# Gate transposes at three to a step, block sums behind two maxima and on GpSimd, in an attention and expert kernel on one core

## The chip, the core and the metric

The kernel runs on one core of a Trainium2 chip. The metric is device time in microseconds of one execution, median of several runs. TensorE (PE) does matrix products and transposes, VectorE (DVE) and ScalarE (ACT) read their results out of PSUM, GpSimd (POOL) works on SBUF alone, and SyncE (SP) issues nearly all loads and stores, in order. Every engine works through its own instructions in program order and waits on semaphores for the others.

## The reference

Two batches of eight heads, 768 positions, head size 64. Each position attends to a band of its neighbours and to 24 blocks of 32 positions, of which the keys are the maximum over the block and the values the mean. The result, 1536 rows of 512, goes through a gate that picks two of eight experts for each row, through these experts, and then through a second feed-forward block.

```python
k_sum = k.reshape(B, H, nb, block, D).max(axis=3)
v_sum = v.reshape(B, H, nb, block, D).mean(axis=3)
mask_l = np.abs(pos[:, None] - pos[None, :]) < window
scores_all = np.concatenate([np.where(mask_l, scores_l, -1e9), scores_s + np.log(block)], axis=-1)
attn = softmax(scores_all) @ np.concatenate([v, v_sum], axis=2)      # x: 1536 x 512
noisy = x @ w_gate + np.log1p(np.exp(x @ w_noise)) * noise           # top two of eight
for each expert e: out[rows of e] += weight * (relu(x[rows] @ w1[e]) @ w2[e])
h = relu(out @ w_in); result = (s * h * h + b) @ w_out
```

## The kernel before

**Attention.** Two heads make a unit `u` (eight units, four to a batch), half of the positions of a unit make a group `n` (16 groups, `u, g = divmod(n, 2)`). The loop over `n` is a software pipeline, one group a step. In step `n` TensorE gets, in this order, the scores of group `n` (`stage_s`, here S(n)), the transposes of the probabilities of group `n-2` (`stage_pt`, pt) and the product with the values of group `n-3` (`stage_pv`, pv). VectorE takes the row maximum of S(n) (L737) and negates and scales it (L738), ScalarE the six exponentials (`stage_exp`, L741) and the copies of the transposes out of PSUM (L755). VectorE normalises pv into the rows of x, `xs[b]` (L771, L773). After a batch's last unit each group's rows are also stored to `x_d` by SP (L776).

For the unit to come, VectorE takes the block maxima of K (`block_max`, L707), GpSimd lays out the windows of K (L703) and places the maxima (L711). `make_vsum` (L688) sums the blocks of `vT` on VectorE; the sums `vz` ride along in `stage_pt` as a seventh transpose (L754), and `place_vsum` puts them into the value tile `VW` (ACT L692, POOL L693). The loads K, Q, vT of unit `u+2` and VW of `u+1` are issued by SP in `extra(n)` at the end of every even step; each waits until its buffer is free.

**PSUM.** `bank()` hands out two banks (`mbk`) in turn to pt (two a step) and to all other short work. The scores alternate between `bk23` and `bk45`; the gate's logits (`gps`) are columns 400 to 495 of `bk23`.

**Gate.** `gate_t(b, i)` transposes 128 rows of x (four transposes, L783) into a bank and copies them to a tile `xt` (ACT L789 or DVE L787). `gate_m(b, k)` multiplies three of these with the gate weights (24 matmuls, L799) and copies the 96x128 result `lt` (ACT L803). `gate_z(b, k)` transposes it back into `bk23` (L806). The table `GATE` places the work of batch 0 in steps 10 to 12, and `TAIL` names that of batch 1 (g, m, z).

**Routing.** `top2`, `ranks`, `slots` (lines 172 to 268) turn logits into slots: many small VectorE operations, for batch 0 spread by `ROUTE` over steps 12 to 15. `first_ids` (d.0, L283 on TensorE, L876 and L877 on VectorE) makes the ids of unit 0's rows, and GpSimd gathers them from `x_d` (L547). `first_x` (x.0, x.1) transposes 128 of these rows each (L528) and splits them into a high (L530) and a low part (L531).

**Tail.** The string `TAIL` is the written order of everything from the last three groups' pt and pv to the first matmuls of unit 0: l1.i and l2.i are the two expert products of step i (L501, L522), s.i splits weights (ACT L411, then L494 and L495 on GpSimd or VectorE), t, r, o, i are the routing of batch 1, whose ids let unit 1's rows be gathered (p.0 to p.3 transpose them). From unit 1 on the loop `step(n)` runs products on TensorE to the end.

Of the kernel before, what the change touches and what calls it, by code (L numbers as in the profile page):

```python
# [9 lines left out]
F32 = mybir.dt.float32  # L10
# [5 lines left out]
AF = mybir.ActivationFunctionType  # L16
# [3 lines left out]
DRAM = bass.MemoryType.DRAM  # L20

EDGE_CAP = 256
GATE_EV = {(0, 1): 1, (0, 3): 1, (0, 5): 1, (1, 0): 1, (1, 3): 1, (1, 4): 1}
CHUNK_AT = (3, 7, 12)
SPLIT_AT = (6, 8)
SPLIT_DVE = {8: 1, 9: 1, 4: 0}
ROUTE = {12: 2, 13: 3, 14: 7, 15: 6}
GATE = {(10, 0): 't0', (10, 1): 't1', (10, 2): 't2', (11, 0): 't3 m0', (11, 1): 't4', (11, 2): 't5 z0', (12, 0): 'm1', (12, 1): 'z1'}
XT_B = 4
TAIL = ("pt.1 pv.0 d.0 pt.2 pv.1 g.0 g.1 pv.2 g.2 g.3 m.0 x.0 g.4 z.0 x.1 s.2 g.5 m.1 l1.0 z.1 s.3 l1.1 t.0 s.4 l2.0 l1.2 u.0 c.3 l2.1 s.5 "  # L30
        "r.0 o.7 l2.2 o.2 s.6 l1.3 l1.4 l2.3 o.2 s.7 l1.5 l2.4 c.4 i.0 l1.6 s.8 l1.7 s.9 l2.6 l2.5 p.0 p.1 e.0 p.2 p.3 l2.7 l1.8")
MID_CAPS = (464, 440, 424, 416, 392, 368, 344)

# [2 lines left out]
def kernel(ctx: ExitStack, tc, q, k, v, vt_in, w_gate, w_noise, noise, w1, w2,  # L36
# [8 lines left out]
    P = 128  # L45
# [490 lines left out]

    def gather_x(u):
        if u == 0:
            t = ap_.tile([P, 2, Dm], F32, name="xg0")
            rows = [t[:, i] for i in range(2)]  # L540
        else:
            t = sp.tile([P, 4, Dm], F32, name="xg", bufs=2)
            rows = [t[:, i] for i in range(4)]
        xg[u] = rows
        for st in range((caps[u] + P - 1) // P):
            w = min(P, caps[u] - st * P)
            nc.gpsimd.indirect_dma_start(  # L547
                out=rows[st][0:w], out_offset=None, in_=x_d[0:S if u == 0 else N, :],
                in_offset=bass.IndirectOffsetOnAxis(ap=ids_i[0:w, 4 * u + st:4 * u + st + 1], axis=0))
# [228 lines left out]
    xt_of = {}  # L778

    def gate_t(b, i):  # L780
        xp = bank()
        for t in range(DT):
            nc.tensor.transpose(xp[:, t * P:(t + 1) * P], xs[b][:, i, t * P:(t + 1) * P], ident)  # L783
        xt = ap_.tile([P, DT, P], F32, name="xt", bufs=XT_B)
        xt_of[b, i] = xt
        if GATE_EV.get((b, i), 0):
            nc.vector.tensor_copy(xt.rearrange("p t n -> p (t n)"), xp)  # L787
        else:
            nc.scalar.activation(xt.rearrange("p t n -> p (t n)"), xp, AF.Copy)  # L789


    gps = bk23[:, :, 400:400 + 96].rearrange("p k (i e) -> p k i e", e=32)
# [2 lines left out]
    def gate_m(b, k):  # L795
        ps = bank()[0:96, 0:P]
        for t in range(DT):
            for j in range(3):
                nc.tensor.matmul(ps[32 * j:32 * j + 32], wgn[:, t], xt_of[b, 3 * k + j][:, t], start=t == 0,  # L799
                                 stop=t == DT - 1)  # L800
        lt = ap_.tile([96, P], F32, name="lt", bufs=2)
        lt_of[b, k] = lt
        nc.scalar.activation(lt, ps, AF.Copy)  # L803

    def gate_z(b, k):
        nc.tensor.transpose(bk23[:, k, 400:400 + 96], lt_of[b, k], ident[0:96, 0:96])  # L806
# [388 lines left out]
```

## Time and profile before

| | us |
|---|---|
| median of 3 runs (690.10 to 690.83) | 690.42 |
| the profiled execution | 686.93 |
| its span, first to last instruction | 685.2 |
| TensorE busy (95%) | 653.4 |
| VectorE busy (63%) | 434.4 |
| ScalarE busy (52%) | 355.6 |
| GpSimd busy (24%) | 164.4 |

Times in the trace are microseconds from the start of the span. A group L737 is what line 737 of the kernel issues. "idle before" is the time in which the engine had nothing to do ahead of the instruction, and the arrow names what ended it. The granted clock (PEclk) is the share of TensorE's 2.4 GHz. The span has an attention part up to about 71 us, a tail up to about 85, unit 0 with the routing of batch 1 up to about 119, and then matrix products.

### The profile page before, as it was taken

The numbers are of one execution on the slowest core, as the hardware profiler recorded it, in microseconds if no ns is written. First come the engines' busy times: TensorE is split into PE (matmuls) and PEld (weight loads), VectorE is DVE, ScalarE is ACT, GpSimd is POOL, SyncE is SP. The second block draws the span as 40 slices with busy tenths as digits, with TensorE's granted clock in tenths as the row PEclk, the third lists the DMA queues.
The fourth block names the chain that finished last, engine by engine and source line by source line (L and its number), as shares of the span: only waits on it lengthen the run. The fifth ranks groups of instructions, "written<-read, shape, count | busy, mean of one in ns | idle before, by whom it ended". The sixth has DMA issues, their size and how long they took to land.

```text
span 685.2 us, 11202 instructions
## 1 busy us (share of the span) xinstructions
PE 653.4 (95%) x4236; PEld 571.8 (83%) x4236; DVE 434.4 (63%) x771; ACT 355.6 (52%) x660; POOL 164.4 (24%) x182
## 2 busy tenths in 40 slices
PE   4997689999999999999999999999999999999996
PEld 4776577889999999999898887888888888888884
DVE  5877466467776676677767666788555565554542
ACT  4866334455445555555555575566444554544432
POOL 5652467004041131303131174502400000000000
PEclk9999989999999999999999999999999999999999
DMA  8994504946566566566666642510410000100001
GB/s 338 378 329 169 186 26 139 354 136 207 183 191 205 172 230 202 183 220 226 204 230 214 223 124 80 163 34 31 124 63 0 1 0 1 63 0 1 0 1 66
DMA packets 58408, 97.58 MB, mean 142 GB/s; under 512 B 6695, under 2 KB 33319, under 8 KB 58347
## 3 DMA queue, kind: packets, MB, share of 16 engines
q1 hardware_dynamic: 54203, 83.62, 35.7%
q0 software_dynamic: 4144, 13.18, 6.8%
q8 instruction: 35, 0.57, 0.4%
q14 instruction: 26, 0.21, 0.1%
HBM read 83.61 MB, written 13.17 MB: 141 GB/s over the span
## 4 chain that ended last, share of the span: by engine, by line
PE 90%; DVE 4%; ACT 2%; DMA 1%; issue 1%; POOL 0%; SPq 0%; ACTq 0%; DVEq 0%
PE sbk L501 40%; PE bk L522 25%; PE bk L923 14%; PE mbk L528 2%; PE bk L768 2%; PE mbk L751 2%; PE mbk L522 1%; PE bk L726 1%; PE mbk L954 1%; DMA xl<-in_vT_dram 1%; ACT sm L741 1%; PE mbk L799 1%; DMA xg<-x_d,ids_i 1%; PE mbk L783 1%; DVE xs L773 0%
## 5 line engine op out<-in xcount | busy, mean ns | idle before, releaser
L501 PE MATMUL sbk<-xh,w 128*128 128x512 f32 (+8 forms) x960 | 280.0, 357 | 0.0
L501 PEld LDWEIGHTS sbk<-xh,w 128*128 128x128 f32 x960 | 176.5, 189 | 19.6 <-ACT xh L530 0.4
L501 PE MATMUL sbk<-xl,w 128*128 128x512 f32 (+8 forms) x480 | 171.0, 356 | 0.2 <-DVE xl L531 0.2
L522 PE MATMUL bk<-w,hh 128*128 128x512 f32 (+2 forms) x512 | 160.9, 396 | 0.0
L411 ACT ACTIVATE w<-r 128x512 fp32r<-128x512 f32 x140 | 80.7, 624 | 91.4 <-PE bk L923 56.9
L522 PEld LDWEIGHTS bk<-w,hh 128*128 128x128 f32 (+2 forms) x512 | 93.4, 188 | 17.9
L461 POOL TENSOR_TENSOR cl<-cl,cp 128x512 f32<-128x512 f32 x32 | 41.3, 1290 | 249.1 <-DVE cp L460 231.1
L522 PE MATMUL bk<-w,hl 128*128 128x512 f32 (+2 forms) x256 | 100.6, 393 | 0.0
L501 PEld LDWEIGHTS sbk<-xl,w 128*128 128x128 f32 x480 | 90.9, 189 | 10.3 <-DVE xl L531 0.5
L923 PE MATMUL bk<-hh,w 128*128 128x464 f32 (+4 forms) x320 | 96.4, 362 | 0.0
L494 DVE TENSOR_TENSOR w<-r,w 128x512 fp32r<-128x512 f32 x64 | 44.2, 690 | 35.2 <-ACT w L411 34.7
L512 ACT ACTIVATE yr<-sbk 128x512 f32<-128x512 f32 x48 | 28.7, 597 | 71.3 <-PE sbk L501 71.3
L517 DVE SCALAR_TENSOR_TENSOR hl<-yr,sb_in,hh 128x512 fp32r<-128x512 f32 x48 | 40.0, 833 | 36.0 <-ACT hh L514 36.0
L513 DVE SCALAR_TENSOR_TENSOR yr<-yr,sb_in 128x512 f32<-128x512 f32 x48 | 36.0, 750 | 41.9 <-ACT yr L512 41.9
L923 PEld LDWEIGHTS bk<-hh,w 128*128 128x128 f32 x320 | 59.8, 188 | 2.5
L514 ACT ACTIVATE hh<-yr,sb_in 128x512 fp32r<-128x512 f32 x48 | 34.8, 725 | 45.9 <-DVE yr L513 45.9
L486 DVE TENSOR_TENSOR w<-wres,w 128x1024 fp32r<-128x1024 f32 x36 | 44.1, 1224 | 22.0 <-ACT w L485 22.0
L522 PEld LDWEIGHTS bk<-w,hl 128*128 128x128 f32 (+2 forms) x256 | 48.0, 187 | 11.5 <-DVE hl L517 0.8
L923 PE MATMUL bk<-hl,w 128*128 128x464 f32 (+4 forms) x160 | 56.9, 356 | 0.0
L505 ACT ACTIVATE hh<-sbk 128x256 fp32r<-128x256 f32 (+7 forms) x72 | 34.5, 480 | 40.0 <-PE sbk L501 37.6
L506 DVE SCALAR_TENSOR_TENSOR hl<-sbk,hh 128x256 fp32r<-128x256 f32 (+7 forms) x72 | 38.9, 541 | 15.5 <-ACT hh L505 15.3
L485 ACT ACTIVATE w<-wres 128x1024 fp32r<-128x1024 f32 x39 | 41.3, 1058 | 14.3 <-PE bk L522 9.6
(186 smaller groups left out, 802.4 us busy)
## 6 DMA issues: line engine op xcount, KB each, us to landing
r<-in_moe_w_dram SPq DMA_DIRECT2D x72, 512.0 KB, 4.6
c<-in_moe_w_in_dram SPq DMA_DIRECT2D x16, 512.0 KB, 3.8
c<-in_moe_w_out_dram SPq DMA_DIRECT2D x16, 512.0 KB, 3.7
VW<-in_v_dram SPq DMA_DIRECT2D x8, 780.0 KB, 8.0
y_d<-yr SPq DMA_DIRECT2D x23, 256.0 KB, 2.3
kT<-in_k_dram SPq DMA_DIRECT2D x8, 384.0 KB, 6.8
qT<-in_q_dram SPq DMA_DIRECT2D x8, 384.0 KB, 8.1
xl<-in_vT_dram SPq DMA_DIRECT2D x8, 384.0 KB, 7.3
```

The source lines that it names most:

```text
L411: nc.scalar.activation(dst, src, AF.Copy)
L461: nc.gpsimd.tensor_tensor(out=lf, in0=lf, in1=pw.bitcast(F32), op=OP.mult)
L485: nc.scalar.activation(v2[:, 0], w, AF.Copy)
L486: eng.tensor_tensor(out=v2[:, 1], in0=w, in1=v2[:, 0].bitcast(F32), op=OP.subtract)
L494: eng.tensor_tensor(out=v4[:, 2], in0=a, in1=v4[:, 0].bitcast(F32), op=OP.subtract)
L501: nc.tensor.matmul(ps, wgt[:, t], x[:, t], start=i == 0, stop=i == 3 * DT - 1)
L506: nc.vector.scalar_tensor_tensor(out=hl, in0=ps, scalar=0.0, in1=hh.bitcast(F32), op0=OP.max, op1=OP.subtract)
L513: nc.vector.scalar_tensor_tensor(out=r2, in0=r, scalar=sb_in[:, 0:1], in1=r, op0=OP.mult, op1=OP.mult)
L514: nc.scalar.activation(hh, r2, AF.Identity, bias=sb_in[:, 1:2])
L517: nc.vector.scalar_tensor_tensor(out=hl, in0=r2, scalar=sb_in[:, 1:2], in1=hh.bitcast(F32), op0=OP.add, op1=OP.subtract)
L522: nc.tensor.matmul(a, g, wgt, start=first and j == 0, stop=last and j == 2)
L923: nc.tensor.matmul(a[:, 0:C], wgt[:, c], x[:, 0:C], start=f == 0 and j == 0, stop=last and j == 2)
```

## The change

**Transposes.** `gate_t(n)` now transposes, for one group, the 128 columns of one unit: three transposes (one for each 128 rows of the group) into three quarters of a bank, and one 128x384 copy into `XT[b]`, on VectorE for odd groups, on ScalarE for even ones. It stands at the end of step `n+4` for groups 0 to 11, and in the tail as v.0 to v.3 for groups 12 to 15 (v.2's copy goes to VectorE). `XT[0]` is a tile of its own; `XT[1]` is the memory of `xs[0]`, so its writers wait for `x_d`'s stores of batch 0. `gate_m` reads `XT` and copies `lt` on VectorE. In `GATE` the products of batch 0 stand in steps 11 and 12, the second gate_z behind pv and the new transposes of step 12.

**Start.** In steps 0 and 1 the maxima and exponentials come right behind the scores, and `make_vsum(0)` follows the second maximum. `load_vT(2)` goes from step 0 to step 1.

**Block sums of units 6 and 7.** GpSimd adds halves in place, five `tensor_tensor` of 24x16, 24x8, 24x4, 24x2 and 24x1 elements a row.

**Tail.** x.0 and x.1 come earlier, x.0 ahead of pv(15) (pv.2); l1.0 comes ahead of m.1 and z.1. The gathered rows of unit 0 go into `kw[0]` instead of a tile of their own.

```diff
-GATE = {(10, 0): 't0', (10, 1): 't1', (10, 2): 't2', (11, 0): 't3 m0', (11, 1): 't4', (11, 2): 't5 z0', (12, 0): 'm1', (12, 1): 'z1'}
-TAIL = ("pt.1 pv.0 d.0 pt.2 pv.1 g.0 g.1 pv.2 g.2 g.3 m.0 x.0 g.4 z.0 x.1 s.2 g.5 m.1 l1.0 z.1 s.3 l1.1 t.0 s.4 l2.0 l1.2 u.0 c.3 l2.1 s.5 "
+GATE = {(11, 1): 'm0', (11, 2): 'z0', (12, 1): 'm1', (12, 2): 'z1'}
+TAIL = ("pt.1 v.0 pv.0 d.0 pt.2 v.1 pv.1 x.0 v.2 pv.2 m.0 x.1 z.0 v.3 s.2 l1.0 m.1 z.1 s.3 l1.1 t.0 s.4 l2.0 l1.2 u.0 c.3 l2.1 s.5 "
...
-            t = ap_.tile([P, 2, Dm], F32, name="xg0")
+            t = kw[0].rearrange("p j c -> p (j c)")[:, 0:2 * Dm].rearrange("p (i d) -> p i d", d=Dm)
...
-        nc.vector.tensor_reduce(z[:, 96:KW], t, AX.X, OP.add)
+        if u < NU - 2:
+            nc.vector.tensor_reduce(z[:, 96:KW], t, AX.X, OP.add)
+            return
+        w = 16
+        while w:
+            dst = t[:, :, 0:w] if w > 1 else z[:, 96:KW, None]
+            nc.gpsimd.tensor_tensor(out=dst, in0=t[:, :, 0:w], in1=t[:, :, w:2 * w], op=OP.add)
+            w //= 2
...
-    def gate_t(b, i):
-        xp = bank()
-        for t in range(DT):
-            nc.tensor.transpose(xp[:, t * P:(t + 1) * P], xs[b][:, i, t * P:(t + 1) * P], ident)
...
+    XT0 = ap_.tile([P, 2, DT, 3, P], F32, name="XT0")
+    XT = [XT0, xs[0].rearrange("p i (a n) -> p (i a) n", n=P).rearrange("p (k t j) n -> p k t j n", k=2, t=DT)]
+
+    def gate_t(n, eng=None):
+        u, g = divmod(n, 2)
+        b, hp = divmod(u, HP)
+        xp = bank()[:, 0:3 * P].rearrange("p (j n) -> p j n", n=P)
+        for j in range(3):
+            nc.tensor.transpose(xp[:, j], xs[b][:, 3 * g + j, hp * P:(hp + 1) * P], ident)
+        if eng or g:
+            nc.vector.tensor_copy(XT[b][:, g, hp], xp)
         else:
-            nc.scalar.activation(xt.rearrange("p t n -> p (t n)"), xp, AF.Copy)
+            nc.scalar.activation(XT[b][:, g, hp], xp, AF.Copy)
...
-        nc.scalar.activation(lt, ps, AF.Copy)
+        nc.vector.tensor_copy(lt, ps)
...
-                load_vT(u + 2)
+                if u:
+                    load_vT(u + 2)
...
         if n == 1:
+            load_vT(2)
             route_consts()
...
-        if n == 0:
+        if n < 2:
+            stage_exp(n)
+        if n == 1:
             make_vsum(0)
-            stage_exp(0)
-        if n == 1:
...
-        if n:
+        if n >= 2:
             stage_exp(n)
...
+        if n >= 4:
+            gate_t(n - 4)
         gate_ops(n, 2)
         extra(n)
```

## Rows read from the trace of the kernel before

**Rows 1.** Busy us by stretch (length; PE, PEld, DVE, ACT, POOL; PEclk; DMA)

```profile
19.06:36.90 17.84, 16.68 (x403) 14.37 (x399) 15.63 (x30) 15.33 (x52) 12.95 (x14) 1.00 0.98 340
36.90:55.47 18.57, 15.03 (x277) 12.18 (x274) 9.91 (x19) 11.82 (x39) 8.75 (x9) 0.97 0.93 338
55.47:71.22 15.75, 11.51 (x239) 9.90 (x238) 14.80 (x53) 8.65 (x28) 6.14 (x7) 0.93 0.34 118
71.22:85.42 14.20, 11.65 (x147) 9.10 (x147) 5.24 (x11) 5.17 (x10) 4.11 (x5) 0.88 0.68 224
85.42:118.69 33.27, 28.36 (x182) 24.77 (x182) 20.33 (x62) 14.07 (x30) 22.73 (x23) 0.90 0.24 73
118.69:685.20 566.51, 559.99 (x2818) 492.66 (x2816) 358.44 (x569) 291.79 (x478) 99.84 (x83) 1.00 0.39 126
```

**Rows 2.** Timeline of the start (start us, us, engine, line, idle before)

```profile
8.28 0.35 PE L729 MATMUL bk<-mask,identb 64*64 64x120 bf16 x4
...
8.98 0.95 DVE L688 TENSOR_REDUCE vz<-xl 128x24 f32<-128x768 f32 x1 [3.77 <-DMA xl<-in_vT_dram]
...
10.87 0.94 DVE L707 TENSOR_REDUCE ks<-kT 128x24 f32<-128x768 f32 x1
...
12.77 0.68 PE L726 MATMUL bk<-kw,qT 64*64 64x120 f32 x8 [2.21 <-POOL kw L711]
...
14.67 0.92 DVE L737 TENSOR_REDUCE bk<-bk 128x6 f32<-128x720 f32 x1 [0.98 <-ACT sm L741]
```

**Rows 3.** Issue to landing of vT(0) and vT(1), line 679

```profile
L679 SPq DMA_DIRECT2D xl<-in_vT_dram x2: 432/446/460, 2.7 to 3.6; - x2
...
DMA to landing us min/median/max: 6.3/7.3/8.3
```

**Rows 4.** Timeline of the gate's work in steps 9 to 12

```profile
37.85 0.66 PE L783 MATMUL mbk<-ident,xs 128*128 128x128 f32 x4
...
39.24 0.59 PE L751 MATMUL mbk<-ident,sm 128*121 128x128 f32 x3 [0.41 <-ACT xt L789]
...
43.17 1.07 PE L799 MATMUL mbk<-xt,wgn 128*32 128x128 f32 x24
...
53.82 0.30 PE L806 MATMUL bk<-ident,lt 96*128 96x96 f32 x1 [2.15 <-ACT sm L741]
```

**Rows 5.** Groups, 19 to 39 us: xcount, busy us, mean ns, idle before

```profile
L755 ACT ACTIVATE PT<-mbk 121x384 f32<-121x384 f32 x13 | 6.1, 497 | 2.1 <-PE mbk L751 1.3 <-PE mbk L754 0.7
...
L773 DVE TENSOR_TENSOR xs<-bk,rc 128x384 f32<-128x384 f32 x7 | 3.9, 557 | 0.2
```

**Rows 6.** Timeline: GpSimd's windows of unit 7 and their load

```profile
51.44 1.15 POOL L703 COPY kw<-kT 128x1152 f32<-128x1152 f32 x1 [3.25 <-DMA kT<-in_k_dram]
```

**Rows 7.** Timeline: first routing operation, maximum of step 13, first ids

```profile
57.15 0.20 DVE L181 TENSOR_TENSOR t<-t,nz_in 128x48 f32<-128x48 f32 x1
...
58.05 0.89 DVE L737 TENSOR_REDUCE bk<-bk 128x6 f32<-128x720 f32 x1
...
71.22 0.54 PE L283 MATMUL bk<-oha,ohb 128*128 128x36 f16 x12 [2.92 <-DVE xs L773]
```

**Rows 8.** Timeline: the same VectorE multiply beside GpSimd

```profile
89.39 1.29 POOL L495 TENSOR_TENSOR w<-r,w 128x512 fp32r<-128x512 f32 x1
...
89.49 1.25 DVE L181 TENSOR_TENSOR t<-t,nz_in 128x48 f32<-128x48 f32 x1
```

**Rows 9.** Timeline of the tail: gather, pv(14), x.0, routing of batch 1

```profile
72.50 1.19 POOL L547 DMA_INDIRECT xg<-x_d,ids_i  x1 [1.26 <-DVE ids_i L877]
...
73.14 1.57 PE L768 MATMUL bk<-VW,PT 121*64 121x65 f32 x24
...
79.50 0.66 PE L528 MATMUL mbk<-ident,xg 128*128 128x128 f32 x4
...
88.98 0.20 ACT L179 ACTIVATE t<-bk 128x48 f32<-128x48 f32 x1
```

**Rows 10.** Issue to landing of unit 0's two gathers, 72 to 82 us

```profile
DMA to landing us min/median/max: 3.9/3.9/4.0
```

More of the change, by code (lines that the diff above doesn't have):

```diff
@@ L22 @@
 EDGE_CAP = 256
-GATE_EV = {(0, 1): 1, (0, 3): 1, (0, 5): 1, (1, 0): 1, (1, 3): 1, (1, 4): 1}
 CHUNK_AT = (3, 7, 12)
@@ L27 @@
 ROUTE = {12: 2, 13: 3, 14: 7, 15: 6}
-GATE = {(10, 0): 't0', (10, 1): 't1', (10, 2): 't2', (11, 0): 't3 m0', (11, 1): 't4', (11, 2): 't5 z0', (12, 0): 'm1', (12, 1): 'z1'}
-XT_B = 4
-TAIL = ("pt.1 pv.0 d.0 pt.2 pv.1 g.0 g.1 pv.2 g.2 g.3 m.0 x.0 g.4 z.0 x.1 s.2 g.5 m.1 l1.0 z.1 s.3 l1.1 t.0 s.4 l2.0 l1.2 u.0 c.3 l2.1 s.5 "
+GATE = {(11, 1): 'm0', (11, 2): 'z0', (12, 1): 'm1', (12, 2): 'z1'}
+TAIL = ("pt.1 v.0 pv.0 d.0 pt.2 v.1 pv.1 x.0 v.2 pv.2 m.0 x.1 z.0 v.3 s.2 l1.0 m.1 z.1 s.3 l1.1 t.0 s.4 l2.0 l1.2 u.0 c.3 l2.1 s.5 "
         "r.0 o.7 l2.2 o.2 s.6 l1.3 l1.4 l2.3 o.2 s.7 l1.5 l2.4 c.4 i.0 l1.6 s.8 l1.7 s.9 l2.6 l2.5 p.0 p.1 e.0 p.2 p.3 l2.7 l1.8")
@@ L776, in stage_pv @@
             nc.sync.dma_start(x_d[r0:r0 + 384, :].rearrange("(i p) d -> p i d", p=P), xs[b][:, 3 * g:3 * g + 3])
-    xt_of = {}
-    def gate_t(b, i):
-        xp = bank()
-        for t in range(DT):
-            nc.tensor.transpose(xp[:, t * P:(t + 1) * P], xs[b][:, i, t * P:(t + 1) * P], ident)
[L784 to L787, printed above, removed]
+    XT0 = ap_.tile([P, 2, DT, 3, P], F32, name="XT0")
[8 more added lines that the diff above has]
+            nc.vector.tensor_copy(XT[b][:, g, hp], xp)
         else:
-            nc.scalar.activation(xt.rearrange("p t n -> p (t n)"), xp, AF.Copy)
+            nc.scalar.activation(XT[b][:, g, hp], xp, AF.Copy)
     gps = bk23[:, :, 400:400 + 96].rearrange("p k (i e) -> p k i e", e=32)
@@ L798, in gate_m @@
             for j in range(3):
-                nc.tensor.matmul(ps[32 * j:32 * j + 32], wgn[:, t], xt_of[b, 3 * k + j][:, t], start=t == 0,
+                nc.tensor.matmul(ps[32 * j:32 * j + 32], wgn[:, t], XT[b][:, k, t, j], start=t == 0,
                                  stop=t == DT - 1)
@@ L809, in gate_ops @@
         for w in GATE.get((n, place), "").split():
-            {"t": gate_t, "m": gate_m, "z": gate_z}[w[0]](0, int(w[1]))
+            {"m": gate_m, "z": gate_z}[w[0]](0, int(w[1]))
     load_k(0)
@@ L1128 @@
     ops = {"pt": lambda i: stage_pt(NG - 3 + i), "pv": lambda i: stage_pv(NG - 3 + i), "x": first_x, "l1": l1, "l2": l2,
-           "g": lambda i: gate_t(1, i), "m": lambda i: gate_m(1, i), "z": lambda i: gate_z(1, i), "s": lambda i: split_step(i, nc.vector if SPLIT_DVE.get(i, 0) else nc.gpsimd),
+           "v": lambda i: gate_t(NG - 4 + i, i == 2), "m": lambda i: gate_m(1, i), "z": lambda i: gate_z(1, i), "s": lambda i: split_step(i, nc.vector if SPLIT_DVE.get(i, 0) else nc.gpsimd),
            "c": load_chunk, "t": route_top2, "u": end_attention, "r": route_ranks, "o": route_slots, "i": route_ids,
```

## The prediction

> **What bounds the kernel now.** I read the busy time by stretch first [rows 1]. From 118.69 us to the end (566.51 us) TensorE is busy 559.99 us and the change touches nothing there, so that stretch only moves as a block, by as much as the first matmul of unit 1 moves. The 33.27 us before it (85.42 to 118.69) are matmuls of unit 0 beside the routing of batch 1; its start, too, is handed down from the left. So the question is how much earlier the work at 85.42 and the routing behind it can start. To the left there are four stretches of different kinds. In steps 4 to 9 (S(4) at 19.06 to S(10) at 36.90, 17.84 us) TensorE has 16.68, VectorE 15.63 and ScalarE 15.33 us busy: three engines nearly full. In steps 10 to 12 (18.57 us) none of them is: TensorE 15.03, VectorE 9.91, ScalarE 11.82. There the gate's transposes, their copies and the waits between them stretch three steps to twice the length of the ones before. From 55.47 to 71.22 VectorE has 14.80 of 15.75 us: the batch 0 routing runs on it beside the attention. In the tail up to 85.42 (14.20 us) TensorE, VectorE and ScalarE take turns. The DMA share is 0.98 and 0.93 up to 55.47, so loads can set a floor as well.
>
> **The change part by part.** All shifts are after minus before, at the named point.
>
> *First block sums behind two maxima.* Now the first maximum waits for the first block sum, which waited 3.77 us for its load and ended at 9.93, though S(1) had been over since 8.63 [rows 2]. Afterwards VectorE does maximum, block maximum of unit 1 and maximum by about 10.0 (0.92 + 0.95 + 0.92 and two small ones, from S(0)'s end, 1.5 us before S(1)'s), then block sum 0 to 11.0, then block sum 1. That one finds vT(1) only at 11.9: issued at 3.6, landed 8.3 us later [rows 3], so it ends at 12.9. S(2) had waited 2.21 us for unit 1's block maxima, which stood behind that first maximum and now end near 9. PE's transpose behind block sum 0, about 0.5 us, lets S(2) start at 11.5, not 12.77, and the third maximum at 13.1, not 14.67 [rows 2]. I take -1.4. Bounds: 0 (the loads of units 2 and 3 land no sooner and absorb it) and -1.6. load_vT(2) goes one step later on SP's queue and waits there for block sum 0, until 11.0 instead of 9.9; K(3), queued behind it, had to wait for the block maximum of unit 1 anyway, until 11.8 before [rows 2], so it loses nothing.
>
> *Three transposes to a step.* Four gate transposes took 0.66 us [rows 4], some 0.3 of it the latency of one (the single small transpose there took 0.30), so 0.12 each and 0.37 for three. The copy of 128x384 out of PSUM is not in the trace; nearest are 0.50 us on ScalarE (121x384) and 0.56 on VectorE (128x384 with a multiply) [rows 5]. Steps 4 to 9 get six of these: TensorE 16.68 + 2.2 = 18.9 us, VectorE 15.63 + 1.7, ScalarE 15.33 + 1.5. Only TensorE passes the 17.84 us. The surcharge is 0.2 us a step if its present gaps close and 0.37 if they stay. Between these and the upper end lies the rotation: a step now takes three banks out of two, so the transposes of P one step later wait for the gate copy, which on ScalarE stands behind six exponentials. Wholly in series that is 0.37 + 0.56 and another 0.5 of waiting, 1.4 us a step. I take 0.37, nearest to the balance of the busy sums: +2.2 in six steps. S(10) comes at 36.90 - 1.4 + 2.2 = 37.7.
>
> *Steps 10 to 12 lose their gate block.* Six evictions and 24 transposes go; three groups' transposes stay (10.0 us for three steps of 17.84/6 + 0.37). Added are two gate products (1.07 us each [rows 4]) and two small transposes (0.30 each [rows 4]). The second small transpose waited 2.15 us for the exponentials of step 12 with pv(9) queued behind it; it is moved behind pv(9) and the new transposes, where I leave 0.3 us of that wait; behind it now stands S(13). Its evacuation goes to VectorE, where it is at most the 0.56 us of the larger copy, in a stretch that is half empty. Sum 13.0: S(13) at 50.75, not 55.47, -4.7. The floor by loads: K(7) freed GpSimd at 51.44 after 3.25 us of waiting [rows 6]. The block maximum of unit 7 needs it too (0.94), the first small routing operations follow (0.9 from L181 to the maximum of step 13, [rows 7]), so that maximum can start at about 53.3; it started at 58.05. Both ways give -4.7. K(7) stands on SP's queue behind the store of x that waits for pv(7); with S(10) only 0.8 later and no gate work between, that store goes out at the same time. Gate copies of batch 1 are written into xs[0], so they wait for the two stores ahead of K(7); ScalarE reaches the first at about 50; 0 to 1.5 us, I take 0.
>
> *Steps 13 to 15, VectorE's stretch.* Out goes one block sum (0.95, [rows 2]); in come two copies (1.1). The block sum of unit 7 becomes five adds on GpSimd, 744 elements in a row: by the 1.29 us of a 512-element subtract there [rows 8] about 2 us, and at most 6.5 if each costs as much as that. They fall beside the routing's VectorE operations. The trace shows what this does: the 48-element multiply L181 took 0.20 us alone [rows 7] and 1.25 beside a GpSimd subtract [rows 8]. I take 0.7 us for three or four such meetings (0 to 2.0). Step 15's transposes wait for the ScalarE copy of step 14 behind its exponentials, which holds up pv(12) and so VectorE: 0.6. Together +1.5: first ids at -3.2. The Trainium skill, page "SBUF — State Buffer", section "Who interferes with whom", says that a VectorE instruction with two SBUF inputs and a GpSimd instruction that reads SBUF share an exclusive lock, and that the second to come is blocked for the whole of the other. L181's two rows agree with it. By it alone the meetings would cost up to the adds' 2 us, and the sum would be 1.3 us worse.
>
> *Tail.* Twelve of its 24 transposes and two evictions are gone, and x.0 stands ahead of pv(15). From the ids (71.22) the first gather is issued 1.28 us later and lands 3.9 after that [rows 9, 10]: x.0 can start 5.2 after the ids; pv(14) ended 3.5 after them, with one gate transpose group added 4.0. Before, x.0 started only at 79.50, 8.3 after. From x.0 to the first expert product it was 5.9 us (to 85.42) with g.4, g.5 and m.1 in between; now v.2, pv(15), m.0, z.0 and v.3 are, and I leave 5.7: 10.9 after the ids instead of 14.2. But m.1 and z.1 now stand behind l1.0 (1.1, and 0.6 of waiting for the copy between them), so routing starts (L179) 16.2 after the ids instead of 17.76 [rows 9]: -1.5. Putting x.0's rows into kw[0] costs nothing, since S(13) is long over. From there both the routing and the products run as before, 1.5 and 3.3 us being the two ends for what this part gives.
>
> **The sum.** -1.4 + 2.2 - 5.5 (18.57 to 13.0) = -4.7 at S(13), which the load floor also gives; + 1.5 - 1.5 leaves -4.7. The profiled execution took 686.93 us with a span of 685.2; its median in the runs is 690.42. A shift this early carries into each alike: span 680.5, execution 682.2, median 690.42 - 4.7 = 685.7.
>
> **Rivals.** *The spread costs more than the block gave back* (slower). Place: steps 4 to 12. With s the surcharge per step, S(13) moves by 9 s - 8.0 (s = 0.37 gives -4.7). Stretch 13 to 15 and the tail cancel, so the kernel is slower from s = 0.9 on; at the 1.4 of full series it is +4.6: 695. For it: the transposes of P already waited on the ScalarE copy in step 10 (0.41 us [rows 4]), and all three engines are full. Against: the busy sums leave TensorE alone over the old length, by 1.1 us in six steps.
> *Loads set the pace.* If step 10 ends 2.5 us later than I think, the store goes out later, K(7) behind it, and the floor rises with it: the maximum of step 13 at 55.8, 688.2. For it: DMA share 0.98. Against: before, that maximum came 6.6 us after K(7) had landed.
> *x.0 blocks TensorE.* It stands in order ahead of pv(15), v.2 and m.0. If the gather lands 4 us later than 3.9 (the first loads took 6 to 8 us [rows 3]), the tail's gain turns into a loss and 689.7 is left. Against: that stretch is past, the share is 0.34 before the tail.
> *The reorder does nothing:* the start's -1.4 vanishes in loads and the lock costs 2.0: 688.4.
>
> **Chances.** Forecast 0.58 (its own range 683.4 to 687.4). Loads, or a reorder that does nothing, 0.14. Gather late 0.09 (0.04 of it faster, 0.04 within 0.2%, 0.01 slower). Spread slower 0.14 (of it 0.04 within 0.2%). Better than 683.4, if routing's meetings with GpSimd fall away and more of the tail's 3.3 us is kept, 0.05. About 0.2% (1.4 us) is what a measurement of this kernel can tell from no change. Faster 0.81, same 0.08, slower 0.11. Range 682.8 to 689.8: it holds forecast, loads and late gather.
>
> **What would show it.** Right: S(2) near 11.5; steps 4 to 9 about 20 us; S(13) near 51 without the 2.15 us wait; the maximum of step 13 right behind K(7)'s block maximum; GpSimd adds beside lengthened L192 to L200; x.0 5 to 6 us after the ids; L179 near 84. Wrong: P transposes waiting on gate copies in each step, S(10) past 42, K(7) landing after 54, or TensorE idle ahead of x.0.

## The result, and the profile of the changed kernel

The changed kernel took 682.28 us (median of 4 runs, 680.78 to 684.72) against 690.26 us for the kernel before beside it: 0.989 of it, interval 0.9856 to 0.9924, or -8.0 us where -4.7 was forecast. Two later comparisons, on two chips, gave 0.9921 (0.9892 to 0.9950) and 0.9892 (0.9873 to 0.9912). All three intervals share 0.9892 to 0.9912, some 6 to 7.5 us. The changed kernel took 682.28, 683.35 and 681.50 us in the three; the kernel before took 690.26 us in the first comparison and 688.05 to 688.88 in the four later ones. So the direction and the order of size were right, but the measured time lies 0.5 us below the forecast's range (682.8 to 689.8), and the forecast's gain was too small.

The profiled execution of the changed kernel took 684.72 us with a span of 683.0, the longest of its four; the forecast for the span was 680.5. The code has moved by a few lines: the scores are L731 (726 before), the maximum L742 (737), the transposes of P L756 (751), pv L773 (768), the first routing multiply L179 (181), the first ids L281 (283), x.0 L526 (528), the block sums L687 and, on GpSimd, L692.

Busy time by stretch of the changed kernel (stretch, length, then busy us and count of PE, PEld, DVE, ACT and POOL, granted clock, DMA share, GB/s), cut at the same pieces of work as [rows 1]: S(4), S(10), S(13), first ids, first expert product, first product of unit 1.

```profile
17.66:38.22 20.56, 19.82 (x417) 16.27 (x417) 16.86 (x34) 17.09 (x57) 14.03 (x16) 1.00 0.96 340
38.22:51.46 13.24, 12.05 (x259) 9.88 (x258) 8.72 (x19) 9.33 (x32) 9.04 (x11) 1.00 1.01 370
51.46:71.10 19.64, 15.38 (x251) 12.63 (x250) 16.71 (x53) 10.49 (x33) 9.72 (x13) 0.83 0.42 158
71.10:81.71 10.61, 7.95 (x108) 6.36 (x108) 3.80 (x11) 2.12 (x5) 2.15 (x3) 0.84 0.53 175
81.71:115.30 33.59, 29.34 (x206) 24.47 (x206) 22.78 (x65) 14.98 (x31) 26.21 (x24) 0.95 0.41 124
115.30:683.00 567.70, 560.13 (x2818) 492.71 (x2816) 359.68 (x569) 291.69 (x477) 99.73 (x82) 1.00 0.38 125
```

The second line is what the change was made for: steps 10 to 12 shrink from 18.57 to 13.24 us. The first pays for it with 2.72 us. The third is 3.89 us longer than before, with VectorE at 16.71 us and the clock at 0.83; the fourth is 3.59 us shorter. What they add up to at S(13), -4.0, is down to -0.1 at the first ids (-0.5 and -1.4 in the profiles of again and after_b, two later runs of the same kernel).

The timeline of the start and of step 5 (start us, us, engine, line, tiles; in brackets the idle time before and what ended it), against [rows 2] and [rows 4]:

```profile
9.08 0.90 DVE L742 TENSOR_REDUCE bk<-bk 128x6 f32<-128x720 f32 x1
10.10 0.94 DVE L687 TENSOR_REDUCE vz<-xl 128x24 f32<-128x768 f32 x1
...
11.40 0.44 PE L731 MATMUL bk<-kw,qT 64*64 64x120 f32 x8
...
...
22.03 0.53 ACT L797 ACTIVATE XT<-mbk 128x384 f32<-128x384 f32 x1
22.61 0.59 PE L756 MATMUL mbk<-ident,sm 128*121 128x128 f32 x3 [0.19 <-ACT XT L797]
```

S(2) starts at 11.40 (forecast 11.5), with both maxima over before the first block sum begins. In step 5 the second half of the transposes of P waits 0.19 us for the gate's copy. Two more such waits follow in steps 4 to 9, of 0.27 us each: the rotation of three banks bites, but by 0.7 us in six steps.

Steps 13 to 15 and the tail of the changed kernel, the timeline, against [rows 6, 7, 9]:

```profile
52.21 0.95 DVE L712 TENSOR_REDUCE ks<-kT 128x24 f32<-128x768 f32 x1 [0.41 <-DMA kT<-in_k_dram]
54.21 0.90 DVE L742 TENSOR_REDUCE bk<-bk 128x6 f32<-128x720 f32 x1
56.14 1.47 POOL L698 COPY VW<-vs 25x1536 f32<-25x1536 f32 x1 [2.39 <-DMA VW<-in_v_dram]
56.39 1.32 DVE L190 TENSOR_TENSOR sel<-z_all,mx 128x96 f32<-128x96 f32 x1
57.68 2.48 POOL L692 TENSOR_TENSOR xl<-xl 128x384 f32<-128x384 f32 x4
57.74 1.06 DVE L191 TENSOR_TENSOR sel<-sel,e 128x96 f32<-128x96 f32 x1
59.93 0.18 PE L218 MATMUL bk<-mm_b,utri 128*128 128x48 bf16 x1 [1.49 <-DVE mm_b L196]
64.64 1.57 PE L773 MATMUL bk<-VW,PT 121*64 121x65 f32 x24
66.26 0.20 DVE L776 RECIPROCAL rc<-bk 128x6 f32<-128x6 f32 x1 [1.76 <-PE bk L773]
71.10 0.47 PE L281 MATMUL bk<-oha,ohb 128*128 128x36 f16 x12 [1.49 <-DVE xs L778]
...
76.01 0.63 PE L526 MATMUL mbk<-ident,kw 128*128 128x128 f32 x4 [1.99 <-DMA kw<-x_d,ids_i]
78.05 1.93 PE L807 MATMUL mbk<-xs,wgn 128*32 128x128 f32 x24
87.50 0.20 ACT L177 ACTIVATE t<-bk 128x48 f32<-128x48 f32 x1
88.01 0.21 DVE L179 TENSOR_TENSOR t<-t,nz_in 128x48 f32<-128x48 f32 x1
92.28 0.20 PE L218 MATMUL mbk<-mm_b,utri 128*128 128x48 bf16 x1 [0.90 <-DVE mm_b L196]
```

The reader sees one chain here. The routing's L190 begins 0.25 us after GpSimd's copy (L698) has begun and ends 0.10 us after its end. L191 begins 0.06 us after the first of GpSimd's adds (384 elements a row, 1.00 us of the 2.48) and ends 0.12 us after its end. The ranks on TensorE wait 1.49 us for the result. Then, in this execution, the clock falls (next view), pv(12) takes 1.57 instead of 0.92 us, and VectorE idles 1.76 us for it. Later x.0 holds TensorE for 1.99 us, the clock falls again and the gate product takes 1.93 instead of 1.07 us [rows 4]. The meetings and the waits come back in the profiles of again and after_b (L190 1.31 and 1.34 us, the ranks 1.48 and 1.47, x.0 2.00 and 2.03), and so does the lower clock behind x.0. Behind the ranks it does not: there the clock stayed at 1.00 for the next 5.5 us in again and up to x.0 in after_b.

Busy time around that wait in the changed kernel (columns as above):

```profile
57.00:60.00 3.00, 1.51 (x32) 1.23 (x31) 2.86 (x6) 0.72 (x2) 2.68 (x5) 1.00 0.81 286
60.00:67.00 7.00, 6.15 (x78) 5.20 (x78) 4.96 (x20) 4.65 (x16) 1.86 (x3) 0.53 0.01 2
67.00:71.00 4.00, 2.48 (x34) 1.86 (x32) 3.93 (x14) 1.39 (x3) 2.70 (x4) 0.96 0.02 4
```

TensorE is busy half of three microseconds and then runs seven at 0.53, near the lower level of 1.2 GHz.

### The profile page after: what moved, and what is told of

It is laid out like the page before. It is cut to its first block, busy times and chain, and to the rows that moved or that the text cites. A ratio compares the mean times of both kernels' runs of the same rounds, so it can differ in the third digit from the quotient of the medians.

```text
span 683.0 us, 11221 instructions
## 1 busy us (share of the span) xinstructions
PE 654.5 (96%) x4236; PEld 570.8 (84%) x4236; DVE 438.6 (64%) x776; ACT 355.0 (52%) x657; POOL 170.8 (25%) x192
## 3 DMA queue, kind: packets, MB, share of 16 engines
HBM read 83.61 MB, written 13.17 MB: 142 GB/s over the span
## 4 chain that ended last, share of the span: by engine, by line
PE 85%; DVE 6%; DMA 5%; issue 1%; ACT 1%; POOL 1%; POOLq 0%; DVEq 0%; ACTq 0%
PE sbk L499 39%; PE bk L520 24%; PE bk L933 14%; PE mbk L526 3%; DMA kT<-in_k_dram 3%; PE mbk L520 2%; PE mbk L964 1%; DMA xl<-in_vT_dram 1%; PE bk L773 1%; DVE bk L742 1%; PE mbk L756 1%; DMA kw<-x_d,ids_i 1%; DVE yT L989 0%; DMA xg<-x_d,ids_i 0%; PE mbk L807 0%
```

## The experiments

Five questions: how large the gain is, which part carries it, what the long steps 13 to 15 cost, what the new tail gives, and what the clock does. Each ratio is to the kernel before on the same chip, with its interval.

| kernel | median us | before us | ratio | interval |
|---|---|---|---|---|
| again, the changed kernel | 683.35 | 688.20 | 0.9921 | 0.9892 to 0.9950 |
| m1_first | 684.07 | 688.20 | 0.9930 | 0.9910 to 0.9949 |
| b_tail | 687.90 | 688.20 | 0.9993 | 0.9980 to 1.0007 |
| b_start | 687.58 | 688.20 | 0.9987 | 0.9973 to 1.0000 |
| vsum_dve | 682.04 | 688.05 | 0.9916 | 0.9894 to 0.9938 |
| x0_late | 683.29 | 688.05 | 0.9929 | 0.9913 to 0.9944 |
| early_act | 682.30 | 688.05 | 0.9910 | 0.9896 to 0.9924 |
| nolock | 683.58 | 688.05 | 0.9924 | 0.9906 to 0.9942 |
| warm | 682.40 | 688.38 | 0.9912 | 0.9889 to 0.9936 |
| early_warm | 682.34 | 688.38 | 0.9913 | 0.9893 to 0.9933 |
| b_warm | 688.46 | 688.38 | 1.0001 | 0.9988 to 1.0013 |
| spread_only | 684.28 | 688.38 | 0.9943 | 0.9923 to 0.9962 |
| after_b, the changed kernel | 681.50 | 688.88 | 0.9892 | 0.9873 to 0.9912 |
| spread_start | 681.16 | 688.88 | 0.9894 | 0.9874 to 0.9914 |
| spread_only_b | 682.95 | 688.88 | 0.9915 | 0.9898 to 0.9933 |
| vsum_ea | 681.48 | 688.88 | 0.9897 | 0.9878 to 0.9917 |

**How large the gain is** (again, after_b; the kernel unchanged).

> The changed kernel once more, for a second profile of it. Theory A (the extra gain sits in the routing of batch 1: VectorE's small operations there meet fewer GpSimd subtracts, TensorE waits 0.90 us for mm_b instead of 3.37 and keeps the full clock): this stretch looks as in the first profile, L177 to the first gather of unit 1 about 17.4 us instead of 20.7. Theory B (the extra gain sits ahead of it, and the first profile fell on an execution that lost it again between 56 and 71 us, where the granted clock fell to 0.69): the first ids come about 67 to 68 us here instead of 71.1, and the stretch from L177 to the gather is again near the 20.7 us of before. Time against before: 0.985 to 0.993 by both.

> The changed kernel once more, beside its parts. It was 8.0 us below the kernel before in the first comparison and 4.9 in the second. If the first was the kernel's size, about 681 us here (ratio 0.989 or less); if the second was, 683 to 684 (0.992 to 0.993).

Measured: -4.9 and -7.4 us by the medians. One kernel, compared three times, came out 0.3% apart, and spread_only, compared twice, also 0.3%. So a single comparison could not tell -5 from -8, and the 0.2% that the prediction gave as what a measurement can tell was too small. Differences under about 2 us between two kernels of the table are not taken as shown below.

**Which part carries it: the spread alone** (spread_only, spread_only_b). The start goes back to the old order, all block sums to VectorE, and the tail to an order that only drops the old transposes.

```diff
-"... pt.2 v.1 pv.1 x.0 v.2 pv.2 m.0 x.1 z.0 v.3 s.2 l1.0 m.1 z.1 s.3 ..."
+"... pt.2 v.1 pv.1 v.2 pv.2 m.0 x.0 v.3 z.0 x.1 s.2 m.1 l1.0 z.1 s.3 ..."
-        if u < NU - 2:
+        if u < NU:
```

> The transposes at three to a step alone: the changed kernel with the start as before, all block sums on VectorE, x.0 behind m.0 and m.1 ahead of l1.0. By the prediction's terms without the start (-1.4), without the adds' meetings (0.7 less the 0.9 of the block sum) and without the reordered tail (some 1.5): scores of group 13 about 3.3 us earlier than before, the time 3 us faster. Rival (the parts only work together; spread alone gives its cost in steps 4 to 9 and loses the rest in VectorE's stretch): 0 to 1 us faster.

> The spread of the transposes alone, on the chip of the whole. About 684.3 (ratio 0.994). Start theory: spread_start lies 0.6 to 1.4 us below it.

Measured: 0.9943 and 0.9915, -4.1 and -5.9 us. This is most of the change.

**Spread and start together** (spread_start: the same, with the new start).

> Spread transposes and the new start, without the GpSimd sums and with x.0 behind m.0 and m.1 ahead of l1.0. By the prediction's sum (the spread and the start carry about 4.2 us to the first ids, tail and sums balance) 683.5 to 684. If the tail order and the sums are worth the 3 us that separate the spread alone from the first comparison of the whole, it stays at 684 and the whole is at 681; if they are worth nothing, the two are within 0.5 us of each other. Its multiply beside GpSimd before the routing's gather should be back at 1.3 us and the 0.5 stretch behind routing of batch 1 with it.

Measured: 0.9894, beside 0.9892 for the whole change on the same chip. The start adds 1.8 us to the spread by the medians, at the edge of what can be told; what is left, the tail order and the GpSimd sums, is worth nothing that can be measured. The busy time by stretch of spread_start (columns as above):

```profile
17.51:38.01 20.50, 19.82 (x419) 16.27 (x417) 16.85 (x34) 17.19 (x57) 14.15 (x16) 1.00 0.98 347
38.01:51.35 13.34, 12.27 (x259) 9.98 (x258) 9.42 (x20) 9.45 (x33) 6.64 (x6) 1.00 1.01 369
51.35:68.21 16.86, 13.95 (x250) 11.60 (x249) 15.37 (x54) 10.78 (x33) 7.32 (x8) 0.90 0.43 165
68.21:78.08 9.87, 7.60 (x132) 6.07 (x132) 4.70 (x12) 2.37 (x5) 2.13 (x2) 1.00 0.64 209
78.08:110.92 32.84, 27.76 (x185) 23.94 (x182) 22.06 (x64) 14.62 (x31) 24.95 (x24) 0.95 0.35 109
110.92:678.70 567.78, 559.98 (x2818) 492.75 (x2816) 358.83 (x569) 291.98 (x478) 99.72 (x83) 1.00 0.39 125
```

Against the changed kernel the third stretch is 2.78 us shorter and the fourth 0.74, although x.0 stands later in it. Four lines of its timeline:

```profile
56.44 0.38 DVE L190 TENSOR_TENSOR sel<-z_all,mx 128x96 f32<-128x96 f32 x1
...
74.42 0.66 PE L526 MATMUL mbk<-ident,kw 128*128 128x128 f32 x4
...
82.51 1.33 DVE L179 TENSOR_TENSOR t<-t,nz_in 128x48 f32<-128x48 f32 x1
...
89.25 0.20 PE L218 MATMUL mbk<-mm_b,utri 128*128 128x48 bf16 x1 [3.36 <-DVE mm_b L196]
```

L190 takes 0.38 us, x.0 waits for nothing. But the multiply of the second routing is back at 1.33 us and the wait for the ranks at 3.36, as before the change [rows 8].

**The start alone, on the kernel before** (b_start: the exponentials of step 1 ahead of `make_vsum(0)`, `load_vT(2)` in step 1).

```diff
-        if n == 0:
-            make_vsum(0)
-            stage_exp(0)
+        if n < 2:
+            stage_exp(n)
         if n == 1:
+            make_vsum(0)
```

> The kernel before with the start alone of the change (two maxima ahead of the first block sum, vT(2) loaded a step later). The prediction: scores of group 2 start 1.3 us earlier and the time falls by 1.4 us (ratio 0.998). Rival: the loads of later units land no sooner, steps 10 to 12 wait for them, and the time stays within 0.4 us.

Measured: 0.9987 (0.9973 to 1.0000), -0.6 us by the medians, between the 1.4 and the 0.4 of the two views and too near to either to choose. In its profile S(2) stood at 11.44, yet S(13) came only 0.8 us earlier and the end no earlier: in the kernel before, most of this gain was lost on the way in that profile.

**The block sums** (vsum_dve: `if u < NU:`, all on VectorE; nolock: only unit 6's sum stays on GpSimd and its copy into `VW` goes to ScalarE).

> The changed kernel with the block sums of units 6 and 7 back on VectorE. Theory A (the adds on GpSimd block the routing's VectorE operations: L190 to L196 took 3.1 us instead of 1.0 in the first profile, which lost 2 us between the maximum of step 13 and the first ids): L191, L194 and L196 fall back to 0.2 to 0.3 us each, the block sum adds 0.9, and the way from that maximum to the ids shrinks from 16 to 17 us to 15 to 16; up to 1 us faster than the changed kernel. Rival B (the copy into VW, which waits for its load, does the blocking, and the adds only follow it): L190 stays above 1 us, the block sum comes on top, and the time is 0 to 1 us slower.

> The changed kernel with the block sum of unit 7 on VectorE and the copy of unit 6's sums into VW on ScalarE: GpSimd does nothing while the routing's first VectorE operations run. Theory A (meetings with GpSimd): L190 to L196 back at about 1.0 us in all instead of 3.1, plus 0.9 for the block sum; from the maximum of step 13 to the ids 1 us less than in the changed kernel, TensorE's wait for mm_b below 1 us, time 0.5 to 2 us faster. Rival B (the fallen clock alone made that stretch long): no change beyond 0.7 us.

Measured: 0.9916 and 0.9924, no difference from the changed kernel. From the maximum of step 13 to the first ids they took 15.4 and 16.0 us, against 16.9, 16.0 and 15.7 in the three profiles of the changed kernel. Two lines of the timeline of vsum_dve, then three of nolock's (where the transposes of P are L760, their copies L764, and the copy into VW is L701 on ScalarE):

```profile
56.53 1.47 POOL L698 COPY VW<-vs 25x1536 f32<-25x1536 f32 x1 [3.15 <-DMA VW<-in_v_dram]
56.88 1.23 DVE L190 TENSOR_TENSOR sel<-z_all,mx 128x96 f32<-128x96 f32 x1
```

```profile
56.63 1.48 ACT L701 ACTIVATE VW<-vs 25x1536 f32<-25x1536 f32 x1 [2.97 <-DMA VW<-in_v_dram]
57.12 0.25 DVE L190 TENSOR_TENSOR sel<-z_all,mx 128x96 f32<-128x96 f32 x1
...
58.67 1.64 PE L760 MATMUL mbk<-ident,sm 128*121 128x128 f32 x6 [3.24 <-ACT PT L764]
```

Without any GpSimd sum L190 still meets the copy into VW: it begins 0.35 us after it here, 1.20 us after it in spread_start. With nothing on GpSimd (nolock) it takes 0.25 us, so the meeting is the cause of its length. In vsum_dve, where only the adds are gone, the ranks wait 0.34 us instead of 1.49. But in nolock the copy stands ahead of ScalarE's own work: ScalarE sits 2.97 us until the load of VW has landed and then copies for 1.48, TensorE waits 3.24 us for the copies of P, and the stretch is no shorter: one wait in the place of another.

**The gate's copies on ScalarE from step 13 on** (early_act), and this with vsum_dve's edit (vsum_ea).

```diff
+        if n >= 13:
+            gate_t(n - 4, nc.scalar)
...
-        if n >= 4:
+        if 4 <= n < 13:
             gate_t(n - 4)
```

> The changed kernel with the gate transposes of steps 13, 14 and 15 ahead of the transposes of P, and their copies on ScalarE. If VectorE's two copies (1.1 us) and the wait of P's transposes for a copy behind the exponentials (0.85 us in the first profile) lengthen steps 13 to 15 as the prediction says, the first ids come 1.5 to 2 us earlier and the time falls by 1 to 2 us. Rival (the stretch is bound by the routing's meetings with GpSimd and by TensorE's fallen clock): the ids move less than 0.7 us and the time stays within 0.7 us.

> The change with the block sums of units 6 and 7 left on VectorE and, from step 13 on, the gate's copies on ScalarE with their transposes ahead of the P transposes. If the two pieces of steps 13 to 15 add up (each alone took 1.5 to 2 us off the way to the first ids in its profile), it lies 1 to 2 us below the change, about 681 where that is 683. If only the clock of each execution decides below the 1 us level, it is within 0.7 us of the change.

Measured: 0.9910 and 0.9897, again not apart from the changed kernel, though the same piece took 14.9 and 14.0 us. In vsum_ea L190 took 0.25 us and TensorE did not wait for the ranks. Removing up to 2.9 us there (0.9 to 2.9, by which profile of the changed kernel one takes) did not show in the medians.

**The tail** (m1_first: m.1 back ahead of l1.0; b_tail: l1.0 ahead of m.1 in the kernel before; x0_late: x.0 behind m.0).

```diff
 m1_first:  "... v.3 s.2 m.1 l1.0 z.1 s.3 ..."
 b_tail:    "... g.5 l1.0 m.1 z.1 s.3 ..."
 x0_late:   "... v.2 pv.2 m.0 x.0 v.3 z.0 x.1 s.2 l1.0 m.1 ..."
```

> The changed kernel with m.1 put back ahead of l1.0 in the tail, as it was before; nothing else. Theory A: m.1 and z.1 between l1.0 and l1.1 hold the second product back until GpSimd is through with the split s.3, so the routing starts while GpSimd is idle; with m.1 ahead, L179 again meets a subtract (1.2 us instead of 0.2), mm_b comes later against l1.1, TensorE idles about 3 us for it and its clock falls: 2 to 4 us slower than the changed kernel. Theory B: the amount of work ahead of the routing is the same, within 0.7 us of the changed kernel.

> The kernel before with one edit: l1.0 ahead of m.1 in the tail. Theory A: 2 to 4 us faster than before (ratio 0.994 to 0.997), with L181 at 0.2 us and TensorE's wait for mm_b down from 3.37 us to about 1. Theory B: within 0.7 us of before.

> The changed kernel with x.0 behind v.2, pv.2 and m.0 in the tail, so TensorE no longer waits about 2 us for the gather with work queued behind it. By the prediction x.0 ahead lets the low and high parts of x start early: with it late the first product comes 0.5 to 1.5 us later and the time grows by as much. Rival: the 2 us wait in front of x.0 is the bound of the tail, filling it with v.2 and pv.2 brings the first product up to 1 us forward and keeps TensorE's clock from falling at 76 us (four stretches at 0.5 become three): up to 2 us faster.

Measured: 0.9930, 0.9993 and 0.9929. m1_first brought back the multiply at 1.32 us and the 3.37 us wait for the ranks, and lost 0.7 us by the medians, less than can be told. b_tail brought the multiply down to 0.57 but not the wait (3.36), and gained nothing. In x0_late x.0 came 1.3 us later behind the ids than in the changed kernel and the first expert product 1.0 us earlier: against those profiles, having x.0 early bought nothing. Two lines of m1_first:

```profile
86.29 1.32 DVE L179 TENSOR_TENSOR t<-t,nz_in 128x48 f32<-128x48 f32 x1
...
93.03 0.22 PE L218 MATMUL mbk<-mm_b,utri 128*128 128x48 bf16 x1 [3.37 <-DVE mm_b L196]
```

The profile of vsum_dve shows the other half of it. Its tail is the changed kernel's, its x.0 waits as long, but its clock stayed at 1.00 from the first ids (69.26) to unit 1 (110.74), as a line of its timeline and two of its stretches show:

```profile
74.10 0.63 PE L526 MATMUL mbk<-ident,kw 128*128 128x128 f32 x4 [1.92 <-DMA kw<-x_d,ids_i]
```

```profile
69.26:78.48 9.22, 6.52 (x108) 5.26 (x108) 3.79 (x11) 2.11 (x5) 2.16 (x3) 1.00 0.45 156
78.48:110.74 32.26, 27.85 (x206) 23.38 (x206) 22.77 (x65) 14.89 (x31) 25.33 (x23) 1.00 0.43 130
```

Here the first expert product comes 9.22 us after the ids, sooner than in x0_late (9.62) and in spread_start (9.87); in the changed kernel's three profiles, with the lower clock behind x.0, it took 10.5 to 10.6. So an early x.0 costs what the clock behind its wait costs, and without that it gains some 0.4 us. One profile shows this.

**The clock** (warm: extra products of the identity with itself fill TensorE's waits in the changed kernel; early_warm: early_act with these; b_warm: the kernel before with such products at three waits). Nothing reads their results.

```diff
+    def warm(k, ps):
+        for _ in range(k):
+            nc.tensor.matmul(ps[:, 0:P], ident, ident, start=True, stop=True)
-"... v.0 pv.0 d.0 pt.2 v.1 pv.1 x.0 ..."
+"... v.0 pv.0 w.8 d.0 pt.2 v.1 pv.1 w.12 x.0 ..."
```

> The changed kernel with extra products of the identity with itself (none is read) where TensorE waits: 14 ahead of the first block sum's transpose, 8 ahead of the ranks of batch 0, 8 ahead of the first ids, 12 ahead of x.0, 4 ahead of the ranks of batch 1, 4, 4 and 6 ahead of unit 1's transposes, each about 0.12 us. Theory C (the executions of the changed kernel differ, from 679 to 687 us, by how often TensorE's clock falls to the lower level behind these waits; the profile with the clock at 0.997 had a span of 677.4, the ones with 0.987 had 682.6 and 683.0): with the waits filled the clock stays at the upper level, the median comes to 677 to 680 us and the spread shrinks. Rival D (the clock is not what differs, or it falls all the same): the median stays at 682 to 684, or is 1 to 3 us slower by the products added.

> The changed kernel with the gate transposes of steps 13 to 15 ahead of P's and their copies on ScalarE, and the extra products of the identity in TensorE's waits. By theory C it is the fastest of these kernels, 676.5 to 679 us, since the first ids come up to 1.5 us earlier too. By rival D it stays at 682.

> The kernel before with the same kind of extra products in its three longest waits of TensorE: 12 in step 12 ahead of the second small gate transpose, 18 ahead of the first ids, 20 ahead of the ranks of batch 1. Its profiles show three stretches at the lower level (13 us in all), each behind one of these waits. Theory C: two or three of them go, 2 to 4 us faster than before, and what is left between this and the filled changed kernel, 5 to 8 us, is the change without the clock. Rival D: within 0.7 us of before.

Measured: 0.9912, 0.9913 and 1.0001. Over its six executions warm had a mean clock of 0.994 to 0.998 and spans of 679.0 to 683.0 us, mean 680.8 (the changed kernel over 14: 677.8 to 685.0, mean 680.9). Two stretches of its profile (columns as above), then lines of its timeline, where L720 is the added products, each of them two rows:

```profile
60.00:67.00 7.00, 5.16 (x90) 4.41 (x90) 6.01 (x23) 5.04 (x17) 1.95 (x3) 1.00 0.01 4
77.00:81.00 4.00, 3.18 (x54) 2.36 (x51) 2.96 (x7) 1.52 (x4) 0.28 (x1) 1.00 0.53 198
```

```profile
8.52 3.78 PE L720 MATMUL bk<-ident 128*128 128x128 f32 x28
...
73.03 2.94 PE L720 MATMUL sbk<-ident 128*128 128x128 f32 x24
75.81 0.60 PE L526 MATMUL mbk<-ident,kw 128*128 128x128 f32 x4
```

The stretches that had 0.53 and the lower clock of the tail in the changed kernel have 1.00 here; the median did not move. But a product took 0.22 to 0.26 us, not the 0.12 that was expected, and so they overfilled the waits: S(2) came at 12.34 us instead of 11.40, S(4) at 18.07 instead of 17.66, and x.0, with no wait left in front of it, 5.6 us behind the ids instead of 4.9. What the held clock gave back and what the products cost are not separated by these runs: the medians are rival D's, and whether for its reason is not shown.

## Why the forecast missed, and what of it held

The sum can now be laid beside the runs, stretch by stretch (us; the changed kernel in three profiled executions, the first is the one shown above):

| stretch | before | forecast | changed | spread_start | spread_only |
|---|---|---|---|---|---|
| start to S(4) | 19.06 | 17.66 | 17.66, 17.66, 17.36 | 17.51 | 19.71 |
| S(4) to S(10) | 17.84 | 20.04 | 20.56, 20.54, 20.54 | 20.50 | 20.55 |
| S(10) to S(13) | 18.57 | 13.05 | 13.24, 13.24, 13.99 | 13.34 | 13.34 |
| S(13) to its maximum | 2.58 | 2.55 | 2.75, 3.30, 2.17 | 2.05 | 2.05 |
| maximum of 13 to first ids | 13.17 | 14.72 | 16.89, 16.01, 15.71 | 14.81 | 14.43 |
| ids to routing of batch 1 | 17.76 | 16.2 | 16.40, 16.33, 16.36 | 13.79 | 13.78 |
| routing to first gather | 20.69 | 20.69 | 17.40, 17.42, 17.40 | 19.82 | 20.69 |
| gather to unit 1's first product | 9.02 | 9.02 | 10.40, 10.57, 10.34 | 9.10 | 9.15 |
| from there to the end | 566.51 | 566.51 | 567.70, 567.53, 566.23 | 567.78 | 566.90 |

**Right.** The start (-1.40 of -1.4). The spread: 20.5 us for six steps against 20.04, a surcharge of 0.45 a step where I took 0.37; TensorE is the bound with 19.82 of 20.56 us busy, and the waits of the P transposes for gate copies come to 0.7 us in all. The rival that needed 0.9 a step is refuted. Steps 10 to 12 (13.2 against 13.05). The load floor: the block maximum of unit 7 waits for K(7) until 52.21 and the maximum of step 13 comes right behind it and the small routing operations, at 54.21 (forecast 53.3). So the floor was reached: the wait for K(7) is 0.41 us here, 0.96 in again and none in after_b. The rival "loads set the pace", which needed 55.8 for that maximum, did not come (54.21, 54.74 and 54.06).

**Mis-sized: VectorE's stretch.** Forecast +1.5, measured +3.7, +2.8 and +2.5. I had counted GpSimd's adds as the partner in the meetings and left out the copy into VW, which was there all along: it meets L190 (1.32 us instead of 0.38 or 0.25), the adds meet L191 (1.06). By the rule that the prediction gave from the Trainium skill, page "SBUF — State Buffer", section "Who interferes with whom", the sum was 1.3 us worse than mine. The trace agrees with that rule: L190 ended 0.10 us after the copy and L191 0.12 us after the first add. Second, I had no term for what a late result does to TensorE: 1.47 to 1.49 us of waiting for the ranks in the three profiles, and in the first of them a clock of 0.53 behind it and pv(12) 0.65 us longer.

**Wrong in its reason: the tail.** The forecast for the routing's start, -1.5 behind the ids, came true (-1.4), but not for the reason that I gave. I credited x.0's earlier place with the gain. spread_only and spread_start, with x.0 late and m.1 ahead of l1.0, need 13.8 us where the new order needs 16.4, and reach the first expert product in 9.87 us instead of 10.6. The gain is that of the removed transposes and evictions alone: m.1 fits into TensorE's wait for the split of x.1 (l1.0 starts 1.59 us behind x.1 with m.1 between them in spread_start, 1.34 without it in vsum_dve), while x.0 ahead of pv(15) makes TensorE wait 1.99 us, at the lower clock afterwards. This is the rival "x.0 blocks TensorE", without any late gather. The clock is more than half of it: in vsum_dve, where it held, the new order needed 15.0 us from the ids to the routing, 1.4 less than in the changed kernel and 1.2 more than in spread_start.

**Wrong: "from there both the routing and the products run as before".** From the routing's start to its first gather it went 3.3 us faster. l1.0 and m.1 in the new order give GpSimd time to finish s.3's subtracts, so the first multiply takes 0.21 us instead of 1.25 [rows 8], the ranks wait 0.90 us, and the clock holds. m1_first, which undoes only that, has 1.32 and 3.37 again: the cause of this piece is shown. The kernel before shows the other side, its busy time in the same place:

```profile
91.00:95.00 4.00, 1.87 (x11) 1.27 (x9) 3.82 (x11) 1.78 (x4) 3.74 (x4) 1.00 0.00 2
95.00:101.00 6.00, 4.77 (x23) 4.19 (x24) 4.25 (x20) 1.15 (x2) 2.62 (x3) 0.51 0.00 1
```

But the 3.3 us do not make up for the 2.6 that the same order costs ahead of the routing and the 1.4 us behind the gather, where TensorE has run out of other products and the clock falls once more (0.79 from 107.00 to 115.30): spread_start reaches unit 1 at 110.92 us without any of it, the changed kernel at 115.30, 115.07 and 113.87. With the clock held the new order is no worse: in vsum_dve the waits behind the gather are there too, but the stretch takes 9.05 us instead of 10.40, and unit 1 starts at 110.74.

**The step that missed the number** is the one from the profile to the median: "a shift this early carries into each alike". In the three profiles unit 1's first product moves by -3.4, -3.6 and -4.8 us, near the -4.7 of the sum. That is luck in part: VectorE's stretch cost 1.0 to 2.2 us more than its term and the way behind the gather 1.3 to 1.6, and the 3.3 us between routing and gather, for which the sum had no term, paid for them. The medians moved by -8.0, -4.9 and -7.4.

Both ends of that last step were off. The profiled execution of the kernel before was a short one: 686.93 us where its median was 690.42, which I stated and then passed over. And the 690.42, from which the 4.7 were taken, came from three long ones (690.10 to 690.83): of 60 later executions, on four chips, two took as long, and their median is 688.27. Whether the chip of the first comparison or chance made them long stays open. Over 60 executions of the kernel before the mean span is 686.66 us (profiled 685.2), over 14 of the changed one 680.87 (profiled 683.0). So two profiles compare a short execution with a long one and show -2.2 us, where the means show -5.8. The forecast of 685.7 was the sum put onto the long three; put onto 688.27 it is 683.6, and the mean of the changed kernel's 14 executions is 682.6.

What makes the changed kernel's executions differ goes with the clock: of its 14, the four with a mean granted clock under 0.989 had spans of 682.4 to 685.0 us, the four at 0.994 and above 677.8 to 680.9. The 60 of the kernel before lie at 0.982 to 0.991 with hardly any relation, at a mean of 0.986; the changed kernel's mean is 0.991. It is tempting to put down to this what the sum still lacks, 1.1 us between its -4.7 and the -5.8 of the means. It is not shown: warm held the clock and was no faster, but its products also delayed the work, and a longer wait lengthens the span by itself. What decides in an execution whether the clock falls behind such a wait, and so the cause of the missing 1.1 us, stays open.

Nothing of the table beats the changed kernel by more than the comparisons can tell. spread_start does as well with two parts fewer.

## What to carry to other kernels

Look up where the profiled execution stands among the runs before a sum made on it is carried to their median, take that median from more than three runs, and give the range that distance. When a change has several parts, ask of each what hides it: here an early x.0 bought a wait with, in each profile of the changed kernel, the lower clock behind it, and m.1, moved behind l1.0, had cost 0.25 us where it stood. The operations on GpSimd were paid for here by VectorE's two-input operations beside them, so list everything that GpSimd runs in that stretch, not only what the change adds.

## What was not expected of the hardware

GpSimd's copy of 25x1536 elements, on 25 partitions only, held up a 128x96 VectorE operation about as long as a subtract of 128x512 does [rows 8]: 1.32 us instead of 0.25. GpSimd's adds by halves got cheaper more slowly than their size, as the groups of the changed kernel between 57 and 62 us show, each shape by itself (busy us, mean ns, then the idle time before):

```profile
L692 POOL TENSOR_TENSOR xl<-xl 128x384 f32<-128x384 f32 x1 | 1.0, 1002 | 0.1
...
L692 POOL TENSOR_TENSOR xl<-xl 128x48 f32<-128x48 f32 x1 | 0.3, 279 | 0.1
L692 POOL TENSOR_TENSOR vz<-xl 128x24 f32<-128x24 f32 x1 | 0.2, 235 | 0.1
```

A sixteenth of the elements takes a quarter of the time, and each add comes with 0.1 us of idle time before it. A wait of 1.49 us on TensorE was followed by seven microseconds at a granted clock of 0.53, in which the same 24 products took 1.57 instead of 0.92 us; the same wait of 1.47 us in after_b was followed by a clock of 1.00.
